# Loading the 64-row remainders of Wq, Wk and Wv over 128 partitions instead of 64

## The chip, the core and the metric

The kernel runs on one core of a Trainium2 chip. The metric is the device time of one execution in microseconds (us). Three executions of the kernel before took 2663.87, 2661.49 and 2657.86 us; the median is 2661.49. A fourth execution was recorded by the hardware profiler; all durations below are from it.

The core has five engines that run their own instruction queues beside each other: TensorE (PE, matrix products; its weight loads are listed as PEld), VectorE (DVE), ScalarE (ACT), GpSimd (POOL) and SyncE (SP). Data come from memory (HBM) through 16 DMA engines, which SP, ACT and POOL feed with transfers. On-chip memory has 128 partitions; a tile's first dimension counts them.

## What is computed

Two pairs of layers over x, which has 2048 rows of 576:

```python
x = x + A(layernorm(x), mem0, Wq, Wk, Wv, Wo)
x = x + B(layernorm(x), w1, w3, w2)
x = x + A(layernorm(x), mem0, Wq, Wk, Wv, Wo)
x = x + B(layernorm(x), w1, w3, w2)
```

`A` is attention over segments of 32 rows. Each segment is put behind a memory of 8 rows, goes through 32 heads of width 128, and its first 8 output rows are the memory of the next segment:

```python
for s in range(n_seg):
    h = concatenate([mem, xs])                # 8 + 32 rows of 576
    q, k, v = h @ Wq, h @ Wk, h @ Wv          # 32 heads of 128 each
    p = softmax(masked(q @ k.T * scale))
    o = (p @ v) @ Wo
    mem = o[:8]; outs.append(o[8:])
```

`B` is a gated feed-forward layer, `(silu(x @ w1) * (x @ w3)) @ w2`, with an inner width of 4608. The weights Wq, Wk and Wv are 576 x 4096 in bfloat16, 4.7 MB each. 576 = 4 x 128 + 64: four chunks of 128 rows and a remainder of 64 rows, 512 KB of each matrix. This remainder is what the change is about.

## The kernel before

The segments are a chain, since each needs the memory of the one before. The kernel walks through 72 steps (64 segments, and the second A layer 8 steps behind the first). In a step, 8 units u of four heads each compute Q and K (QK: the four 128-row chunks; QKt: the 64-row remainder), then scores, softmax, the products with V, and the output product with Wo. FFN work is spread between the steps.

Nothing here is ordered by the hardware alone. `make_nodes` (L232) lists every piece of work with what it depends on; `plan` (L78) puts PE's pieces in the order of a hand-written string of letters (`FIRST`, `FOUR`, `LAST`, L201 to L222: Q is QK, q is QKt) and fits the other engines' work around it. Every instruction of an engine then runs in the order in which the plan emitted it. The lowest-level helpers are `mm` (L632, every matmul), `act` (L635), `v` (L638, every VectorE instruction), `dma` (L641, SP), `adma` (L644, ACT) and `swdma` (L647, POOL), so the profile shows those lines.

The weights are held on chip for the whole run. `T.W` (L1299) has 128 partitions and nine slots of 4096 columns: slots 0 to 3 hold Wq's four chunks, 4 to 7 Wk's, and slot 8 holds both remainders, Wq's 64 rows in partitions 0 to 63 and Wk's 64 rows in partitions 64 to 127. `T.WV` (L1301) holds Wv's chunks and behind them its remainder, which is folded: even blocks of 512 columns in partitions 0 to 63, odd blocks in 64 to 127. The remainder of the activations (`T.HT`, slot 4) is there twice, in both halves of the partitions. So `qk_tail` (L957) can run Q's remainder on the lower and K's on the upper half of PE's rows, as pairs of products of 64 rows each.

Loads at the start, in the order of their queues:

- on ACT: Wk's remainder (64 rows x 8 KB), the first 128 rows of x (XN), mem0 (8 rows), Wv's odd blocks (64 rows x 4 x 1 KB)
- on SP: Wq's remainder (64 rows x 8 KB), Wv's even blocks, then `load_qk` (L693) with the four chunks of the left half of Wq (512 KB each), of Wk's left half, the same of both right halves, `load_v` (L717) with four chunks of 1 MB, `load_o` (L723) with four of 1.15 MB, and the first FFN weights

Each of these transfers signals one of eight semaphores, taken in turn, and a transfer isn't issued before the one eight places earlier has landed. The first step's QK waits for the chunks of Wq and Wk (`ld_h`, L262), its V products for Wv, its output products for Wo.

At the end, the last FFN's weights w1 and w3 are loaded over `T.W` (`tail_load`, L746), 512 columns at a time, after the products of the last step that read those columns (L548); the second and later ones are also held back until named output products.

Of the kernel before, what the change touches and what calls it, by code (L numbers as in the profile page):

```python
# [13 lines left out]
P = 128  # L14
R64 = 64
D = 576
NCH = D // R64
H = 32
E = 128
# [7 lines left out]
NG = 4  # L27
# [204 lines left out]
def make_nodes(em, nseg, pools, o=Opt, dma_bw=230e3, load_bw=345e3):  # L232
# [9 lines left out]
    def banks(n=2):  # L242
        return [Slot("bank") for _ in range(n)]
# [12 lines left out]
    def load(name, nbytes, prio, fn, deps=()):  # L256
        return node("DMA", nbytes / load_bw, fn, deps=deps, prio=prio, name=name, lat=2.0)
# [8 lines left out]
    b = banks(1)  # L266
# [193 lines left out]
    def job(j):  # L460
# [81 lines left out]
        if last:  # L542
            v_done, qk_done = last_reads
            me = steps[nst - 1]
            gates = {1: me["WO1"], **{i: me["WO3"] for i in range(2, 8)}}
            for i in range(8):
                g = gates.get(i)
                tail.append([load("tail", kb(128, c), s0 + o.tail_at + 0.01 * i, em.tail_load(i, what, g), deps=dep + [g])  # L548
                             for what, c, dep in ((0, 9 * 512, qk_done[2 * i:2 * i + 2]), (1, 4 * 576, v_done))])
            shared.pop()()  # L550
        norm()
        if last:
# [29 lines left out]
    for t in range(nst):  # L582
        if t % 4 == 2 and (t + 2) // 4 < ngrp:
            x_in((t + 2) // 4)
        if t == LAG:
            ht_mem[t].append(node("DVE", 0.1, em.init_mem(1, LAG), deps=[m0e] + reads_ht.get(LAG - R_HT, []), prio=LAG - 2, name="m0"))
        if role(t) == 0 or t == 0:
            vx_pair(t - role(t), t - 1 + o.vx)
        step(t)
        if t % 4 == 1 and t // 4 < ngrp:  # L590
            x_res(t // 4)
        if t % 4 == 3:
            job((t + 1) // 4 - 1)
        elif t == nst - 1:
            job(nst // 4)
# [6 lines left out]
SW = 2 * QW  # L602
# [5 lines left out]
class Emitter:  # L608
# [91 lines left out]

    def load_tails(self, what):
        def f(n):
            if what < 2:
                d, wd = (self.dma, self.a.wq) if what == 0 else (self.adma, self.a.wk)
                d(self.T.W[what * R64:(what + 1) * R64, 8, :], wd[4 * P:D, :])
            if what != 1:
                r = what // 2
                (self.adma if r else self.dma)(self.wv(True)[r * R64:(r + 1) * R64, :].rearrange("p (q n) -> p q n", q=NG),
                                               self.a.wv[4 * P:D, :].rearrange("p (q r n) -> r p q n", q=NG, r=2)[r])
        return f  # L710

    def wv(self, tail):
# [227 lines left out]
    def qk(self, t, u, b):  # L940
# [13 lines left out]
                                first and j == 0 and c == 0, c == 3)  # L954
        return f

    def qk_tail(self, t, u, b):  # L957
        def f(n):
            q0, q1 = self.qcols(t)
            HTt = self.ht(t)  # L960
            first = self.begin(b)
            for j in range(4):
                h0 = self.head(u // 2, 4 * (u % 2) + j) * E
                for kind in (0, 1):
                    rr = slice(kind * R64, (kind + 1) * R64)
                    self.mm(self.bk(b[kind])[:, j * SW:j * SW + q1 - q0], self.T.W[rr, 8, h0:h0 + E], HTt[rr, 4, q0:q1],
                            first and j == 0, True, tile_position=(kind * R64, 0))
        return f

    def qk_ev(self, t, u, r, q, b):  # L970
# [420 lines left out]
```

## Time and profile before

| | before |
|---|---|
| median of three executions | 2661.49 us |
| the profiled execution | 2662.86 us |
| its span, from first to last instruction | 2661.1 us |
| PE busy | 2585.4 us (97%) |
| PEld busy | 2228.9 us (84%) |
| DVE busy | 2025.0 us (76%) |
| ACT busy | 1252.0 us (47%) |
| DMA, mean over the span | 140 GB/s |
| DMA in the first of 40 slices (66.5 us) | 321 GB/s |

The page gives the busy time of each engine, then the span in 40 slices, the DMA queues, the chain of work that ended last, and groups of equal instructions. A trace behind it can be asked for a stretch of time: who waited for whom (total, times, longest), the instructions in order of time, the share of the 16 DMA engines that was busy and the rate in GB/s, and how many packets each queue moved. Queue q1 is SP's, q10 is ACT's; a packet is one contiguous piece of a row, and a transfer also ends with small packets, which are counted under 512 B. A share of the DMA engines a little over 100% means that packets overlap on an engine.

### The profile page before, as it was taken

How to read it: one execution, taken by the hardware profiler on the slowest of the kernel's cores; microseconds unless marked ns; L12 is line 12 of the kernel's file. 1: busy time of each engine (PE TensorE's matmuls, PEld its weight loads, DVE VectorE, ACT ScalarE, POOL GpSimd, SP SyncE). 2: the span in 40 equal slices, each digit the busy share in tenths (PEclk: the TensorE clock that was granted, in tenths of full speed). 3: DMA queues.
4: the chain of work that ended last, by engine and by line, in shares of the span. 5: the costliest groups of instructions: out<-in, count | busy, mean ns of one | idle time of the engine just before them, and what ended most of it. 6: DMA issues, size and time to landing. Idle time of an engine off the chain costs nothing.

```text
span 2661.1 us, 134392 instructions
## 1 busy us (share of the span) xinstructions
PE 2585.4 (97%) x59795; PEld 2228.9 (84%) x59795; DVE 2025.0 (76%) x5276; ACT 1252.0 (47%) x3612; POOL 337.1 (13%) x399
## 2 busy tenths in 40 slices
PE   5999999999999999999999999999999999999998
PEld 4788888888888888888888888888888888888887
DVE  4787777787787778777777777777778777777876
ACT  2555453454445444444544444454544445454453
POOL 1111110110111011011101101110111111011110
PEclk8999999999999999999999999999999999999999
DMA  9064845556565556555554655645465564544457
GB/s 321 4 179 123 189 105 149 127 136 148 128 144 105 147 125 145 142 131 147 113 139 116 162 128 141 154 110 136 113 155 125 143 157 101 129 119 128 128 158 236
DMA packets 688135, 371.55 MB, mean 140 GB/s; under 512 B 234072, under 2 KB 682336, under 8 KB 686912
## 3 DMA queue, kind: packets, MB, share of 16 engines
q1 hardware_dynamic: 684016, 355.07, 53.2%
q8 instruction: 467, 7.65, 1.2%
q0 software_dynamic: 3024, 6.93, 0.9%
q10 hardware_dynamic: 512, 0.94, 0.1%
q14 instruction: 116, 0.95, 0.1%
HBM read 306.72 MB, written 2.36 MB: 116 GB/s over the span
## 4 chain that ended last, share of the span: by engine, by line
PE 67%; DMA 7%; DVE 4%; ACT 1%; SPq 1%; issue 1%; POOL 0%; DVEq 0%; POOLq 0%; ACTq 0%
PE bank L632 67%; DMA PTS<-PB 4%; DMA W<-in_B_w_dram 2%; DVE STAT L638 1%; DMA W2C<-in_B_w_dram 1%; DVE SME L638 1%; SPq L641 1%; DVE PB L638 1%; DVE V L638 1%; ACT V L635 0%; DVE XR L638 0%; DVE HTT L638 0%; DVE QKT L638 0%; POOL PB L1052 0%; ACT QKT L635 0%
## 5 line engine op out<-in xcount | busy, mean ns | idle before, releaser
L632 PEld LDWEIGHTS <-W 128*128 128x128 bf16 (+2 forms) x32576 | 1270.4, 101 | 137.4 <-issue 58.6
L632 PE MATMUL bank<-HT,W 128*128 128x80 bf16 (+3 forms) x23040 | 800.0, 197 | 25.9 <-DMA W<-in_A_Wk_dram 8.5
L632 PE MATMUL bank<-XTB,W 128*64 128x256 bf16 (+5 forms) x9536 | 663.2, 263 | 6.3 <-DMA W<-in_B_w_dram 5.9
L1052 POOL MEMSET PB<- 128x1024 bf16 x288 | 273.9, 951 | 1958.6 <-DMA PTS<-PB 1292.0
L635 ACT ACTIVATE QKT<-bank 128x256 bf16<-128x256 f32 (+4 forms) x1456 | 338.9, 310 | 284.6 <-PE bank L632 272.1
L632 PE MATMUL bank<-OT,WO 128*128 128x80 bf16 (+3 forms) x11520 | 417.3, 198 | 1.5 <-issue 0.8
L632 PEld LDWEIGHTS <-WO 128*128 128x128 bf16 (+1 forms) x11520 | 386.2, 102 | 36.8 <-issue 20.9
L635 ACT ACTIVATE V<-bank 64x512 bf16<-64x512 f32 (+1 forms) x625 | 351.7, 585 | 120.2 <-PE bank L632 112.3
L632 PE MATMUL bank<-WV,HT 128*32 128x512 bf16 (+4 forms) x3688 | 370.2, 384 | 1.3 <-DVE HT L638 0.7
L632 PE MATMUL bank<-W2C,HTT 128*64 128x288 bf16 (+1 forms) x3296 | 321.5, 287 | 4.7 <-DMA W2C<-in_B_w_dram 4.7
L635 ACT ACTIVATE OT<-bank 128x320 bf16<-128x320 f32 (+1 forms) x384 | 144.3, 403 | 335.6 <-PE bank L632 332.1
L638 DVE TENSOR_REDUCE STAT<-SME 104x8 f32<-104x320 f32 (+1 forms) x576 | 274.6, 477 | 32.4 <-ACT SME L635 27.0
L638 DVE TENSOR_TENSOR PB<-SME,STAT 40x128 bf16<-40x128 f32 (+4 forms) x912 | 275.5, 336 | 12.2 <-POOL PB L1052 0.4
L638 DVE SCALAR_TENSOR_TENSOR HTT<-HTT,bank 128x512 bf16<-128x512 bf16 (+1 forms) x324 | 201.2, 621 | 105.0 <-ACT HTT L635 101.9
L632 PEld LDWEIGHTS <-HT 128*32 128x32 bf16 (+4 forms) x3688 | 159.0, 100 | 133.3 <-issue 29.7
L632 PEld LDWEIGHTS <-HTT 128*64 128x64 bf16 (+1 forms) x3376 | 230.2, 106 | 42.0 <-issue 8.4
L635 ACT ACTIVATE HTT<-bank 128x512 bf16<-128x512 f32 (+1 forms) x324 | 174.2, 550 | 189.2 <-PE bank L632 187.7
L638 DVE SCALAR_TENSOR_TENSOR XR<-bank,XR 128x288 f32<-128x288 f32 x574 | 242.4, 446 | 18.0 <-PE bank L632 14.9
L635 ACT ACTIVATE SME<-SME 104x320 f32<-104x320 f32 (+1 forms) x288 | 135.2, 469 | 208.1 <-DVE SME L638 205.6
L638 DVE CAST QKT<-bank 128x128 bf16<-128x128 f32 (+2 forms) x592 | 158.2, 315 | 94.5 <-PE bank L632 92.6
L638 DVE TENSOR_TENSOR HTT<-HTT,bank 128x512 bf16<-128x512 bf16 (+1 forms) x324 | 203.5, 628 | 32.5 <-DVE HTT L638 1.4
L638 DVE CAST V<-bank 32x512 bf16<-32x512 f32 (+1 forms) x239 | 163.4, 684 | 33.6 <-PE bank L632 29.4
(59 smaller groups left out, 1414.6 us busy)
## 6 DMA issues: line engine op xcount, KB each, us to landing
W<-in_B_w_dram SPq DMA_DIRECT2D x608, 256.0 KB, 3.9
W2C<-in_B_w_dram SPq DMA_DIRECT2D x304, 288.0 KB, 3.7
W<-in_B_w_dram SPq DMA_DIRECT2D x608, 32.0 KB, 3.8
W<-in_B_w_dram SPq DMA_DIRECT2D x16, 512.0 KB, 8.6
W<-in_A_Wq_dram SPq DMA_DIRECT2D x9, 512.0 KB, 10.2
WO<-in_A_Wo_dram SPq DMA_DIRECT2D x4, 1152.0 KB, 16.7
XR<-in_A_x_dram POOLq DMA_DIRECT2D x16, 288.0 KB, 4.0
WV<-in_B_w_dram SPq DMA_DIRECT2D x8, 576.0 KB, 7.1
```

What stands on the lines that cost most here:

```text
L632: self.ch("PE", self.nc.tensor.matmul(out, lhsT=lhsT, rhs=rhs, start=start, stop=stop, skip_group_check=True, **k))
L635: self.ch("ACT", self.nc.scalar.activation(*a, **k))
L638: self.ch("DVE", getattr(self.nc.vector, fn_)(*a, **k))
L641: self.ch("SP", self.nc.sync.dma_start(out=out, in_=in_))
L1052: return lambda n: self.ch("POOL", self.nc.gpsimd.memset(self.T.PB[:, pb.i], 0.0))
```

## The change

The remainders are loaded in pieces of 128 partitions: one transfer takes two neighbouring blocks of columns of the 64 rows and puts the first into partitions 0 to 63 and the second into 64 to 127. For this the source is read as "h p n": two blocks h, 64 rows p, n columns. The layout of slot 8 changes with it: Wq's remainder takes columns 0 to 2047 in both halves, Wk's columns 2048 to 4095, so that for each unit Q's and K's parts still lie in opposite halves (`qk_tail_at`). Wk's blocks 0 and 3 are still loaded over 64 partitions. Wv's remainder keeps its layout and comes in four transfers. In place of two transfers on SP and two on ACT for the remainders there are four on SP and five on ACT. The loads that overwrite `T.W` at the end depend on the QKt pieces that read the new places.

```diff
@@ make_nodes, the last FFN's loads
-                             for what, c, dep in ((0, 9 * 512, qk_done[2 * i:2 * i + 2]), (1, 4 * 576, v_done))])
+                             for what, c, dep in ((0, 9 * 512, qk_done[2 * i:2 * i + 1] + [me[f"QKt{u}"] for u in range(8) if any(em.qk_tail_at(k, u)[1] == 512 * i for k in (0, 1))]), (1, 4 * 576, v_done))])
@@ load_tails
-            if what < 2:
-                d, wd = (self.dma, self.a.wq) if what == 0 else (self.adma, self.a.wk)
-                d(self.T.W[what * R64:(what + 1) * R64, 8, :], wd[4 * P:D, :])
+            def pair(d, out, wd, at, n):
+                d(out, wd[4 * P:D, at:at + 2 * n].rearrange("p (h n) -> h p n", h=2))
+
+            if what == 0:
+                for i in (0, 1):
+                    pair(self.dma, self.T.W[:, 8, i * 1024:(i + 1) * 1024], self.a.wq, i * 2048, 1024)
+            elif what == 1:
+                self.adma(self.T.W[R64:P, 8, 3072:4096], self.a.wk[4 * P:D, 0:1024])
+                pair(self.adma, self.T.W[:, 8, 2048:3072], self.a.wk, 1024, 1024)
+                self.adma(self.T.W[0:R64, 8, 3072:4096], self.a.wk[4 * P:D, 3072:4096])
             if what != 1:
-                r = what // 2
-                (self.adma if r else self.dma)(self.wv(True)[r * R64:(r + 1) * R64, :].rearrange("p (q n) -> p q n", q=NG),
-                                               self.a.wv[4 * P:D, :].rearrange("p (q r n) -> r p q n", q=NG, r=2)[r])
+                for q in range(what, what + 2):
+                    pair(self.adma if what else self.dma, self.wv(True)[:, q * 512:(q + 1) * 512], self.a.wv, q * 1024, 512)
@@ new function, and qk_tail
+    def qk_tail_at(self, kind, u):
+        i = u // 2
+        block = (3 if i in (0, 3) else 2) if kind else i // 2
+        return R64 * (i % 2 ^ kind), block * 1024 + u % 2 * 512
...
             for j in range(4):
-                h0 = self.head(u // 2, 4 * (u % 2) + j) * E
                 for kind in (0, 1):
-                    rr = slice(kind * R64, (kind + 1) * R64)
-                    self.mm(self.bk(b[kind])[:, j * SW:j * SW + q1 - q0], self.T.W[rr, 8, h0:h0 + E], HTt[rr, 4, q0:q1],
-                            first and j == 0, True, tile_position=(kind * R64, 0))
+                    r0, w0 = self.qk_tail_at(kind, u)
+                    rr = slice(r0, r0 + R64)
+                    self.mm(self.bk(b[kind])[:, j * SW:j * SW + q1 - q0], self.T.W[rr, 8, w0 + j * E:w0 + (j + 1) * E], HTt[rr, 4, q0:q1],
+                            first and j == 0, True, tile_position=(r0, 0))
```

The order of instructions on every engine stays as it was, apart from the loads at the head of SP's and ACT's queues.

## The prediction

> **What bounds the kernel now.** I read the page's busy shares first, then PE's waits by stretch, then the DMA stretches and packet counts of the first 60 us, the only time in which the moved loads run. TensorE (PE) is busy 97% of the span. After 60 us its listed waits add up to some 39 us in 2.6 ms, none of them on Wq, Wk or Wv; before that it waits for these. PE's waits from 13.5 to 58 us:
>
> ```profile
> PE bank L632 <- DMA W<-in_A_Wk_dram: 8.5, 8, 1.1
> PE bank L632 <- DMA W<-in_A_Wq_dram: 4.1, 3, 2.2
> ```
>
> (total us, times, longest.) In time order on PE (start, length, what, idle before it):
>
> ```profile
> 14.85 0.22 PE L632 MATMUL bank<-HT,W 128*128 128x40 bf16 x1 [0.82 <-DMA W<-in_A_Wq_dram]
> 16.13 0.22 PE L632 MATMUL bank<-HT,W 128*128 128x40 bf16 x1 [1.06 <-DMA W<-in_A_Wq_dram]
> 17.41 0.22 PE L632 MATMUL bank<-HT,W 128*128 128x40 bf16 x1 [1.06 <-DMA W<-in_A_Wk_dram]
> 18.70 0.22 PE L632 MATMUL bank<-HT,W 128*128 128x40 bf16 x1 [1.08 <-DMA W<-in_A_Wk_dram]
> ```
>
> One matmul runs each time a 512 KB chunk lands, every 1.28 us: 524,288 B / 1.28 us = 410 GB/s. The DMA stretches (last columns: share of the 16 DMA engines, GB/s) show the same rate, and a slower head:
>
> ```profile
> 2.00:7.00 5.00, 0.00 (x0) 0.00 (x0) 4.30 (x7) 0.00 (x0) 3.67 (x9) 1.00 0.98 225
> 7.00:9.00 2.00, 0.00 (x0) 0.00 (x0) 1.89 (x5) 0.00 (x0) 0.00 (x0) 1.00 1.15 224
> 9.00:13.00 4.00, 0.96 (x15) 0.81 (x16) 1.72 (x8) 1.25 (x1) 0.56 (x1) 1.00 1.04 328
> 14.00:20.00 6.00, 0.92 (x6) 0.45 (x5) 0.00 (x0) 0.00 (x0) 0.00 (x0) 1.00 1.02 407
> ```
>
> The engines are full from 2 us on. The last weight chunk of this queue, WO's fourth, is issued at 44.85 and lands 11.9 us later, at 56.7; PE's WO products run from 51.7 to 57.9 and close the first step. So the stage to 58 us is as long as the load queue: what the queue's head gains or loses reaches step 0's end nearly whole, and as PE's order is written out by hand and it is full from then on, it reaches the end of the kernel.
>
> **What the change does, part by part.** (1) It removes four 64-row transfers (1.573 MB: Wk 512 KB, Wq 512, Wv twice 256). From 2.0 to 13.4 us all queues moved 3.02 MB (the DMA view of that stretch, below); at 407 GB/s that is 7.4 us, so 4.0 us were lost at the head. The four transfers then held the engines 1.573 MB / 407 = 3.9, plus 4.0: **7.9 us**.
>
> (2) It adds seven transfers over 128 partitions (Wq two and Wk one of 256 KB, Wv four of 128 KB: 1,310,720 B) and two of 64 rows (Wk, 128 KB each). What decides is how many DMA engines one of the seven gets. Their source is written "h p n" with h = 2: its outermost step counts two, where every load of before counts 64 or 128 outermost; only the destination counts 128. The trace has one transfer with a small count, mem0's, of 8 rows, on ACT's queue:
>
> ```profile
> DMA packets 1210, 3.02 MB, mean 265 GB/s; under 512 B 120, under 2 KB 768, under 8 KB 1082
> q1 hardware_dynamic: 698, 2.07, 69.6%
> q10 hardware_dynamic: 512, 0.94, 33.6%
> ```
>
> ACT's queue is q10. Its data are Wk's 64 rows of 8 KB, XN's 128 rows, 64 x 4 pieces of 1 KB of Wv and mem0's 8 rows: 456 packets. The other 56 are small closing packets, 56 = 16 + 16 + 16 + 8: each wide transfer was closed by sixteen engines, the 8-row one by eight. So transfers are dealt to engines by their outermost count, and a count under 16 leaves engines out. [...] Each pair is then carried by **two engines**, one half each.
>
> [...]
>
> Price from rows. From 14 to 20 us, 676 packets (80 of them closings) took 102.3% of 16 engines x 6 us: 98.2 us / 596 = 165 ns per 4 KB. From 46.5 to 50.5, 1,353 packets of 1,152 B took 108.6% of 64 us: 51 ns. On the line through both, 2 KB is 86 ns and 1 KB 46 ns. Each of the two engines carries 64 packets per pair: 3 x 64 x 86 = 16.5 us, 4 x 64 x 46 = 11.8 us. The two 64-row transfers give each engine 8 packets of 2 KB; at the head's pace (8 KB in some 560 ns from 2 to 6.9 us, a quarter of it 0.14 us) 1.2 us. New: **29.5 us** on two engines against 7.9 on all: **+21.6 us**. All later chunks need all 16 engines, so they land at the pace of these two.
>
> Bounds: at the pace of 8 KB packets alone on the engines (from 32 to 38 us 301 of them, beside 18 of 4 KB, took 101.8% of 96 us: 315 ns, 26.0 GB/s an engine) 25.2 + 0.65 - 7.9 = +18. At ACT's 1 KB packets from 10 to 12.8 us (202 in 24.9% of 44.8 us: 55 ns, and twice that for 2 KB) 21.1 + 14.1 + 1.2 - 7.9 = +28.5. [...]
>
> (3) New waits. The loads take eight semaphores in turn; mem0 and the two Wv pairs of ACT are now ninth to twelfth and wait, in ACT's queue, for the first Wq pair, the Wk pair and the second Wq pair. Behind them on ACT stand the table load and the copies into HT (11.74 to 14.0 us now). On two engines the second Wq pair is done around 20 to 24 us; HT would follow some 3 us later, XN's own load by 25 at the latest. PE's first full product would start with Wq's first chunk at 29 to 36 us and its first unit end with Wk's fourth chunk, at 21.2 + 21.6 = 43. So these waits lie under the loads: nothing. Without that cover (sixteen engines) the second Wq pair ends by 6 to 7 us, before XN's landing at 8.4: nothing again. Five more issues at 0.35 to 0.6 us lie under the transfers.
>
> (4) QKt (L957) reads the other half for u = 2, 3, 6 and 7, K opposite. The trace's pairs start 3 ns apart and 32 ns after the pair before, in both halves at once; that stays. Where a unit with the other order follows directly, one matmul could wait for its half: written order has 84 such places, so at most 84 x 32 ns = 2.7 us; I take nothing, the nearest row being a pair that already waits 32.
>
> (5) The last FFN's loads over W wait for other QKt. SP's order is unchanged. The first such load is issued at 2594.9 to 2597.4, when six units' QKt of the last step run (2594.98, 48 matmuls); the next at 2609.9, after all of them. Nothing; at worst the first loads slip 1 us, with SP idle till 2599.3 behind.
>
> Sum: the profiled execution took 2662.86 us (span 2661.1 and 1.8 around it), 1.4 above the median 2661.49. 2662.86 + 21.6 = 2684.5, on the median's level 2683.1; I forecast **2684**.
>
> **Rivals.** *Sixteen engines after all (faster, within measurement).* If the destination's 128 rows deal the transfer, the head runs at full width: of the 4.0 us lost, 0.55 stays with the two 64-row Wk transfers (0.26 MB at 225 instead of 407 GB/s) and 0.3 with smaller packets: -3.1 us, 2659.8, on the median's level 2658. For it: 225 GB/s with the engines 98% busy, next to 407. It decides at the outermost count: if the source's 2 doesn't limit. Against: mem0's eight closings. [...]
>
> *Two engines, but another two for each transfer.* Then the busiest engine has one pair, 64 x 86 = 5.5 us, and 1.2: 6.7 instead of 7.9, about -1 us: 2661 to 2662. The packet counts can't show which engines are used.
>
> *Two engines, and part of the delay lost.* PE's granted clock is 0.61 from 32 to 40 us; another start could run at another clock, 2 us either way. It lies inside the range.
>
> **Chances.** Two engines, always the same: 0.80. Sixteen: 0.12. Changing couples: 0.05. Anything else slower: 0.03. The range holds the first: +18 and +28.5 on 2661.5, with 3 us for the spread of the runs (2657.86 to 2663.87): 2676 to 2693. A measurement of this kernel tells 0.2%, 5.3 us, from no change; sixteen engines give -3.1, mostly within it: faster 0.02, same 0.15, slower 0.83.
>
> **What would show it.** Right: from 2 to 30 us a DMA share near 2/16 in long stretches and a mean under 120 GB/s; two closing packets per pair; Wk's fourth chunk used near 43 us, WO's last product near 79; all later rows as before, 22 us later. Wrong: 400 GB/s from the start, with the first full product before 13 us (sixteen engines), or Wk's fourth chunk at 20 to 22 (changing couples). An end that moves without the 58 us mark moving would refute parts 4 and 5.

## The result, and the profile after

The changed kernel took 2682.18 us (median of four executions, 2680.11 to 2683.95); the kernel before took 2660.84 (four, 2657.86 to 2663.87). The ratio is 1.0082, 95% interval 1.0070 to 1.0095: slower by 21.3 us on the medians. The profiled execution took 2683.95 us (span 2682.2), 21.1 more than that of before. The forecast was 2684, in a range of 2676 to 2693.

The stretches of the changed kernel (last three columns: PE's granted clock, share of the 16 DMA engines, GB/s):

```profile
2.00:7.00 5.00, 0.00 (x0) 0.00 (x0) 4.30 (x7) 0.00 (x0) 3.67 (x9) 1.00 0.51 108
7.00:9.00 2.00, 0.00 (x0) 0.00 (x0) 1.34 (x3) 0.00 (x0) 0.00 (x0) 1.00 0.13 51
14.00:20.00 6.00, 0.00 (x0) 0.00 (x0) 0.94 (x3) 0.00 (x0) 0.00 (x0) 1.00 0.13 50
36.00:42.00 6.00, 0.86 (x4) 0.42 (x4) 0.00 (x0) 0.00 (x0) 0.00 (x0) 1.00 0.98 356
```

A share of 0.13 is 2.1 of 16 engines, and they move 50 GB/s where before moved 407 in the same stretch. The DMA view of 14 to 20 us tells more:

```profile
DMA packets 169, 0.30 MB, mean 50 GB/s; under 512 B 9, under 2 KB 37, under 8 KB 169
q1 hardware_dynamic: 108, 0.21, 9.1%
q10 hardware_dynamic: 61, 0.09, 4.1%
```

Both queues, SP's q1 and ACT's q10, have a pair in flight here, and together they fill 13.2% of the engines. With another couple for each transfer it would be four engines, 25%. So it is the same two. The page's row of ACT's queue counts the closing packets:

```profile
q10 hardware_dynamic: 710, 0.94, 0.1%
```

Its data are 64 + 128 + 64 rows of Wk, 128 of XN, 8 of mem0 and 2 x 128 of Wv: 648. The other 62 are 16 each for the three wide transfers, 8 for mem0 and 2 for each of the three pairs. PE in time order (start, length, what, idle before):

```profile
24.13 0.32 PE L632 MATMUL bank<-HT,W 64*128 64x40 bf16 x8 [1.64 <-ACT HT L635]
33.47 0.22 PE L632 MATMUL bank<-HT,W 128*128 128x40 bf16 x1 [9.02 <-DMA W<-in_A_Wq_dram]
35.15 0.22 PE L632 MATMUL bank<-HT,W 128*128 128x40 bf16 x1 [1.47 <-DMA W<-in_A_Wq_dram]
...
43.32 3.51 PE L632 MATMUL bank<-HT,W 128*128 128x40 bf16 x97 [1.08 <-DMA W<-in_A_Wk_dram]
```

Before, the last of these rows was:

```profile
21.24 3.51 PE L632 MATMUL bank<-HT,W 128*128 128x40 bf16 x97 [1.05 <-DMA W<-in_A_Wk_dram]
```

The activations are ready at 24, but Wq's first chunk is used at 33.47 and Wk's fourth at 43.32; before used the latter at 21.24, so the step is 22.1 us late. PE's waits from 13.5 to 80 us put 12.5 us on Wq where before had 4.1:

```profile
PE bank L632 <- DVE XN L638: 21.5, 1, 21.5
PE bank L632 <- DMA W<-in_A_Wq_dram: 12.5, 4, 9.0
PE bank L632 <- DMA W<-in_A_Wk_dram: 8.0, 7, 1.5
```

The 21.5 (counted from the span's start) are the wait for XN, the first rows of x. That load has 128 rows and so sixteen shares, two of which stand behind the pairs (fourteen of its closings come by 6.84 us, the last two at 18.13 and 19.01; 16 of its rows' packets still run after 14 us): issued at 3.03, it lands at 19.01, where before had it at 8.4. This costs nothing of its own, since Wq comes later still. The step ends with WO's products, last start at 79.1 (57.9 before). The changed kernel's row, then before's:

```profile
L632 PE MATMUL bank<-OT,WO x160: 179/202/243, 70.8 to 79.1; 128*128 128x40 bf16 x128, 128*64 128x40 bf16 x32
L632 PE MATMUL bank<-OT,WO x160: 179/186/243, 51.7 to 57.9; 128*128 128x40 bf16 x128, 128*64 128x40 bf16 x32
```

From there the same instructions of the two traces lie 21 to 25 us apart to the end.

### The profile page after: what moved, and what is told of

Read it like the earlier page. It is cut to its first block, busy times and chain, and to the rows that moved or that the text cites. A ratio compares the mean times of both kernels' runs of the same rounds, so it can differ in the third digit from the quotient of the medians.

```text
span 2682.2 us, 134396 instructions
## 1 busy us (share of the span) xinstructions
PE 2584.9 (96%) x59795; PEld 2230.1 (83%) x59795; DVE 2024.8 (75%) x5276; ACT 1253.4 (47%) x3612; POOL 337.4 (13%) x399
## 4 chain that ended last, share of the span: by engine, by line
PE 81%; DMA 9%; DVE 5%; ACT 2%; SPq 1%; issue 1%; POOL 0%; DVEq 0%; POOLq 0%; ACTq 0%
PE bank L632 81%; DMA PTS<-PB 5%; DMA W<-in_B_w_dram 2%; SPq L641 1%; DVE V L638 1%; DVE SME L638 1%; DVE STAT L638 1%; ACT V L635 1%; DMA W<-in_A_Wk_dram 1%; DVE HTT L638 1%; DMA W<-in_A_Wq_dram 1%; DVE PB L638 1%; DMA W2C<-in_B_w_dram 1%; ACT QKT L635 0%; DVE XR L638 0%
## 5 line engine op out<-in xcount | busy, mean ns | idle before, releaser
L632 PE MATMUL bank<-HT,W 128*128 128x80 bf16 (+3 forms) x23040 | 801.3, 197 | 34.2 <-DMA W<-in_A_Wq_dram 12.5
L632 PEld LDWEIGHTS <-WO 128*128 128x128 bf16 (+1 forms) x11520 | 386.8, 102 | 38.5 <-issue 22.5
```

Of the source, the lines that this page charges most:

```text
L632: self.ch("PE", self.nc.tensor.matmul(out, lhsT=lhsT, rhs=rhs, start=start, stop=stop, skip_group_check=True, **k))
```

## The experiments

**Theory:** the transfers' outermost count of two leaves each pair to the same two engines, and the 21 us are the time of their packets. **Rivals:** the new places of the remainders (QKt, the late loads), the number of transfers, or the new waits on ACT hold up the start. Each set has its own runs of the kernel before: their medians are 2660.12 us (25 runs) for the first four kernels, 2657.59 (29) for the next three and 2657.54 (7) for the last.

**1. Each pair cut into two transfers of 64 partitions.** Places, order and bytes stay; the outermost count becomes 64.

```diff
-                d(out, wd[4 * P:D, at:at + 2 * n].rearrange("p (h n) -> h p n", h=2))
+                for h in (0, 1):
+                    d(out[h * R64:(h + 1) * R64], wd[4 * P:D, at + h * n:at + (h + 1) * n])
```

> Each paired transfer of the changed kernel is cut in two transfers of 64 partitions, lower then upper; places, QKt, the later dependencies and the wait rules stay as changed. Theory (each pair is carried by two DMA engines because the source's outermost step counts two): all 16 engines work again, the remainders take 6 to 9 us instead of 29.5, Wk's fourth chunk is used at 19 to 22 us (43.3 in the changed kernel), time within 3 us of the kernel before (2658 to 2664), about 20 us under the changed one. Rival (the loss comes from the new places in W, from QKt's halves or from the new waits on ACT, not from how a transfer is dealt out): still 2676 to 2684, and Wk's fourth chunk after 35 us.

Measured: 2664.92 us (11 runs), ratio 1.0013, interval 1.0003 to 1.0023. The stretches:

```profile
2.00:7.00 5.00, 0.00 (x0) 0.00 (x0) 4.30 (x7) 0.00 (x0) 3.67 (x9) 1.00 0.92 236
7.00:9.00 2.00, 0.00 (x0) 0.00 (x0) 1.89 (x5) 0.00 (x0) 0.00 (x0) 1.00 0.62 138
14.00:20.00 6.00, 0.86 (x4) 0.41 (x4) 0.00 (x0) 0.00 (x0) 0.00 (x0) 1.00 1.01 395
```

With the same places, nearly all of the 0.82% is gone: the delay comes neither from the places nor from the late loads, but from the paired form of the transfers. (Cutting a pair changes its partitions and the number of transfers as well as the outermost count; experiment 2 changes the count alone.) Wk's fourth chunk is used at 23.48, later than expected. The engines have a hole at 7 to 9 us (share 0.62): eight short transfers, where before had two, now stand ahead of Wq's first chunk on SP, which is issued at 8.53 (2.27 in before). A remainder of 0.13% is left; experiments 5 and 6 look for it.

**2. The same pairs with the rows outermost.** The source count becomes 64. The data of a row then land in two neighbouring partitions, so the remainders are not where the products look for them; that other values cost no time is assumed, here and in experiments 3 and 7.

```diff
-                d(out, wd[4 * P:D, at:at + 2 * n].rearrange("p (h n) -> h p n", h=2))
+                d(out, wd[4 * P:D, at:at + 2 * n].rearrange("p (h n) -> p h n", h=2))
```

> The paired transfers read their source as p h n instead of h p n: the same bytes, rows, packets, partitions and issues, only the source's outermost step counts 64 instead of 2. [...] Theory (outermost count): 16 engines, full rate from the start (near 400 GB/s from 3 us on), the head's loss of 4 us mostly gone: Wk's fourth chunk used near 18.2 us, time 1 to 4 us under the kernel before, 2657 to 2660 where it runs at 2661. Rival (the pattern with a third dimension is slow to issue, whatever its order): as the changed kernel, 2680 to 2684. Second rival (128 partitions win nothing over 64): as before within 1 us, Wk's fourth chunk at 21 us.

Measured: 2665.82 us (11 runs), ratio 1.0018, interval 1.0008 to 1.0029. Neither the delay nor the gain that I expected is there. Its stretches:

```profile
2.00:7.00 5.00, 0.00 (x0) 0.00 (x0) 4.30 (x7) 0.00 (x0) 3.67 (x9) 1.00 0.93 254
7.00:9.00 2.00, 0.00 (x0) 0.00 (x0) 1.85 (x5) 0.00 (x0) 0.00 (x0) 1.00 1.05 337
30.00:36.00 6.00, 4.38 (x115) 3.96 (x115) 1.53 (x6) 0.79 (x3) 0.96 (x1) 0.50 1.02 425
52.00:60.00 8.00, 6.11 (x170) 5.78 (x169) 1.15 (x5) 1.28 (x5) 1.62 (x2) 0.50 1.04 281
```

The head is better than before's: 254 and 337 GB/s where before had 225 and 224. Wk's fourth chunk is used 1.0 us earlier (20.20), and from 32 to 56 us the kernel is 2.4 to 3.0 us ahead of before. At 59 us no more than 0.3 us of it is left, and from 64 to 200 us mostly 0.6 to 0.7. From 52 to 60 us PE stands once before WO, and its clock is 0.50 throughout, against 0.79 in before's same stretch. PE's row, then before's stretch and row:

```profile
54.90 2.86 PE L632 MATMUL bank<-OT,WO 128*128 128x40 bf16 x80 [1.41 <-issue]
52.00:60.00 8.00, 7.41 (x243) 7.04 (x240) 2.10 (x9) 1.81 (x8) 2.48 (x3) 0.79 0.92 270
55.85 2.23 PE L632 MATMUL bank<-OT,WO 128*128 128x40 bf16 x80
```

Before ran this block of 80 in 2.23 us, 0.6 less, and did not stand before it. So the width of the transfer alone is not what costs: 128 partitions with 64 rows outermost give back all but 0.18% of 0.82%. How most of the lead of 2.5 us is lost is seen in one profile, as a stop of 1.41 us and a lower clock; that the earlier start brings these about was not tried. It is not the whole of the 0.18%: from 500 us on this trace lies 1.0 to 5.5 us behind before, for which I have no cause, and experiment 1's trace, too, wanders after 60 us, between 2.5 us ahead of before and 2.2 behind.

**3. Four engines.** Count four: 32 rows by four column blocks. The upper 32 rows of the remainders are not loaded and other columns stand in their places, so a part of Q, K and V is computed from wrong weights.

```diff
-                d(out, wd[4 * P:D, at:at + 2 * n].rearrange("p (h n) -> h p n", h=2))
+                at = 0 if n == 1024 else at % 2048
+                d(out, wd[4 * P:4 * P + 32, at:at + 4 * n].rearrange("p (h n) -> h p n", h=4))
```

> The paired transfers take four blocks of 32 rows instead of two of 64: the same bytes, packets and partitions, source's outermost count 4 (the upper 32 rows are left out and other columns stand in their place, so the products of the remainders differ). Theory: four engines, each with 32 packets per transfer: 3 x 32 x 86 ns + 4 x 32 x 46 ns = 14.1 us, with the 1.2 us of the two 64-row ones 15.3 instead of 7.9: 6 to 9 us over the kernel before, 2667 to 2670; DMA share near 4/16 in the head; Wk's fourth chunk near 28.6 us. Rival (engines change from transfer to transfer, or the cost is per transfer and not per engine): over 2677 or under 2664.

Measured: 2673.52 us (4 runs), ratio 1.0049, interval 1.0035 to 1.0063: 13 us over before, more than expected; Wk's fourth chunk is used at 31.31, not near 28.6. The share of engines while only such transfers run is the one expected of four engines, 4/16; the excess lies elsewhere. From 30 to 36 us the engines are not full:

```profile
7.00:9.00 2.00, 0.00 (x0) 0.00 (x0) 1.34 (x3) 0.00 (x0) 0.00 (x0) 1.00 0.27 102
30.00:36.00 6.00, 4.69 (x143) 4.47 (x144) 1.33 (x5) 0.91 (x3) 0.00 (x0) 1.00 0.60 186
```

and SP's waits to 45 us say for what:

```profile
SPq L641 <- DMA WV<-in_A_Wv_dram: 13.9, 4, 6.2
```

SP waits for pairs of Wv whose semaphores it takes again for later chunks, ACT's two among them, which ACT issued late, behind its own wait. Experiment 7 takes this away.

**4. Before, with Wv alone in pairs.** Wq and Wk stay as they were.

```diff
...
+                for q in range(what, what + 2):
+                    (self.adma if what else self.dma)(self.wv(True)[:, q * 512:(q + 1) * 512],
+                                                      self.a.wv[4 * P:D, q * 1024:(q + 1) * 1024].rearrange("p (h n) -> h p n", h=2))
```

> The kernel before with one part of the change alone: Wv's remainder in four paired transfers; Wq, Wk, W's places and QKt as before. Theory: 4 x 64 x 46 ns = 11.8 us on the same two engines in place of some 3 us on all: 7 to 11 us over the kernel before, 2668 to 2672. Rival (each transfer gets another couple of engines): 2.9 us on each couple, within 1 us of before. Rival (places and QKt cost the time): within 1 us of before.

Measured: 2669.52 us (8 runs), ratio 1.0033, interval 1.0018 to 1.0047: some 9 us, as expected. Four of the seven pairs, with 40% of the paired bytes, make about 40% of the delay (0.33 of 0.82%; by the interval 0.18 to 0.47), without any new place for Wq and Wk.

**5. The new places alone.** Slot 8 has the changed layout, with QKt and the last FFN's dependencies as changed; the loads go over 64 partitions, in few transfers.

```diff
-            def pair(d, out, wd, at, n):
-                d(out, wd[4 * P:D, at:at + 2 * n].rearrange("p (h n) -> h p n", h=2))
+            def half(d, out, wd, r):
+                d(out.rearrange("p (q n) -> p q n", q=2), wd[4 * P:D, :].rearrange("p (q r n) -> r p q n", q=2, r=2)[r])
...
```

> The new places in W, QKt's new halves and the last FFN's new dependencies, with loads like those of before: 64 partitions, rows of 2 KB, two transfers for Wq, three for Wk, two for Wv. It asks for the price of the places alone, which the cut-up pairs left at 0.13% together with their 16 transfers. Theory (places and QKt's halves cost nothing, part 4 of the prediction): within 2 us of before. Rival (QKt's unlike neighbours and the later dependencies cost): 3 to 5 us over before, spread over the steps.

Measured: 2657.62 us (12 runs), ratio 0.9998, interval 0.9989 to 1.0008. The places cost nothing, to within some 3 us either way.

**6. The pieces alone.** Before's places, the remainders in 16 transfers of 64 partitions.

```diff
-                d(self.T.W[what * R64:(what + 1) * R64, 8, :], wd[4 * P:D, :])
+                for c in range(0, 4096, 1024):
+                    d(self.T.W[what * R64:(what + 1) * R64, 8, c:c + 1024], wd[4 * P:D, c:c + 1024])
...
```

> The kernel before with its places, and the remainders in the same 16 transfers of 64 partitions as the cut-up pairs (four each for Wk and Wq, eight for Wv). Theory (the 0.13% of the cut-up pairs come from the number of transfers at the head, which moves Wk's fourth chunk from 21.2 to 23.5 us): 2 to 4 us over before, Wk's fourth chunk near 23.5. Rival (the places cost it): within 1 us of before.

Measured: 2658.71 us (12 runs), ratio 1.0006, interval 0.9993 to 1.0018. Wk's fourth chunk is used at 22.15, 0.9 us after before's and not at the 23.5 expected of the theory. From 2 to 7 us these transfers of 64 partitions, with XN's beside them as in experiment 2, move as much as experiment 2's of 128:

```profile
2.00:7.00 5.00, 0.00 (x0) 0.00 (x0) 4.30 (x7) 0.00 (x0) 3.68 (x9) 1.00 0.92 256
```

Neither places nor pieces by themselves can be told from no change, so where the 0.13% of experiment 1 comes from stays open.

**7. Four engines, all pairs of Wv on SP.** Experiment 3, with Wv's four transfers ahead of Wq's first chunk on SP and none on ACT.

```diff
-            if what != 1:
-                for q in range(what, what + 2):
-                    pair(self.adma if what else self.dma, self.wv(True)[:, q * 512:(q + 1) * 512], self.a.wv, q * 1024, 512)
+            if what == 0:
+                for q in range(NG):
+                    pair(self.dma, self.wv(True)[:, q * 512:(q + 1) * 512], self.a.wv, q * 1024, 512)
```

> The kernel with four blocks of 32 rows (products of the remainders differ as there), but all four Wv transfers on SP ahead of Wq's first chunk, none on ACT. With four engines it took 13.4 us over before where 7.4 were worked out, and SP's issue of Wk's fourth chunk (24.67) and Wq's next (31.18) stood behind the landing of ACT's two Wv transfers, whose semaphores they take. Theory (that wait is the difference): the loads no longer stall, Wk's fourth chunk near 29 us, time 6 to 9 us over before. Rival (four engines cost 13 us by themselves): as with the two on ACT, 12 to 14 us over before, and Wk's fourth chunk at 31 us.

Measured: 2663.21 us (10 runs), ratio 1.0021, interval 1.0009 to 1.0034: 5.6 us, where experiment 3 had 13, and a little under the 6 to 9 expected. Wk's fourth chunk is used at 30.30, only 1.0 us before experiment 3's and not near 29; the gain comes behind it. The stretch in which experiment 3 had a share of 0.60 is full, and SP's waits for Wv are short:

```profile
30.00:36.00 6.00, 5.34 (x156) 5.06 (x157) 2.23 (x6) 1.44 (x6) 0.00 (x0) 1.00 1.03 411
```
```profile
SPq L641 <- DMA WV<-in_A_Wv_dram: 5.1, 4, 1.5
```

So with four engines the waits through ACT cost some 7 us (13.4 less 5.6, each known to within 4). The prediction held such waits to be free in the changed kernel; the last experiment asks that.

**8. The changed kernel, all pairs of Wv on SP.** The edit of experiment 7 on the changed kernel, two engines.

> The changed kernel with one difference: all four pairs of Wv are issued by SP ahead of Wq's first chunk, and none by ACT behind mem0, so that nothing on ACT waits for a semaphore of SP's pairs. The seven pairs are the same and still go out on two engines each. Theory A (the new waits of part 3 lie under the loads and cost nothing; the delay is the two engines' own 29.5 us): the median stays 19 to 22 us over before, Wk's fourth chunk is used at 42 to 44 us. Theory B (as with four engines, where the waits on ACT's late pairs took some 7 us of the 13, in the changed kernel too the stall through ACT is a part of the delay): 13 to 17 us over before, Wk's fourth chunk at 36 to 39 us. Between them, 17 to 19 us, a part of it.

Measured: 2675.61 us (4 runs), ratio 1.0071, interval 1.0044 to 1.0098, 18.1 us over before. That lies between the ranges of the two theories, and the interval, 12 to 26 us, doesn't tell them apart. The trace says more. Its stretch and PE's line for Wk's fourth chunk:

```profile
14.00:20.00 6.00, 0.00 (x0) 0.00 (x0) 1.18 (x4) 0.00 (x0) 0.40 (x1) 1.00 0.13 50
```
```profile
41.92 3.51 PE L632 MATMUL bank<-HT,W 128*128 128x40 bf16 x97 [1.07 <-DMA W<-in_A_Wk_dram]
```

41.92 is 1.4 us before the changed kernel's 43.32, just under theory A's 42 to 44 and far from the 36 to 39 of a stall. 0.5 us of it is there at Wq's first chunk (32.97 instead of 33.47), the rest comes from chunks that now land every 1.28 us where the changed kernel has gaps up to 1.7. At two engines the waits lie under the pairs but for some 1.4 us at the first unit, in one profile of each. At the step's end it is 2.6 us (WO's last product starts at 76.5 instead of 79.1); how much of that is the clock's stays open.

## Why the prediction was right

**Parts 1 and 2, the sum.** Right in kind and size. The price per packet fits: from 14 to 20 us the trace has 132 packets of 2 KB, 18 of 1,152 B and 10 of 1 KB, which took 84.8, 52 and 46 ns in the mean; the prediction's line has 86, 51 and 46. By these, 132 x 86 + 18 x 51 + 10 x 46 ns = 12.73 us, and 13.2% of 96 us are 12.67. The pairs' last packet, on ACT's queue, ends at 34.99, 33.0 after the head's start at 2.0. Among the pairs' packets the two engines also carried their shares of XN (8 x 52 ns) and of Wq's first two chunks (16 x 165 ns; landed at 33.42 and 35.11), together 3.1 us. That leaves 29.9; forecast 29.5. From 22.5 to 30 us (share 0.67) the other fourteen engines do their shares of Wq's first chunks, but each chunk lands only when the two get to it: of the first, fourteen closings come from 24.49 to 25.16 and the last two at 31.49 and 33.42; it is used at 33.47, the seven others 1.2 to 1.7 us apart, "at the pace of these two", as forecast. Wk's fourth chunk at 43.32 (forecast near 43) and WO's last product at 79.1 (near 79) follow; the mean from 2 to 30 us is 108 GB/s, under the 120 named.

That the source's count of two alone limits the transfer, which the forecast takes and no row of before showed, is now shown: two closings per pair; a share of 0.27 (four of 16 are 0.25) at count four, in experiment 3 from 7 to 9 us; 0.93 and 1.05 in experiment 2, with the same 128 partitions. Nor did a row of before show that all seven pairs go to the same two engines, on which the 29.5 us rest; the share of 0.13 shows it for the pairs in flight together, and the 29.9 us left above fit it for all seven. Which two of the sixteen they are is not shown.

**Part 3, the waits.** "Nothing" was nearly right for the changed kernel: by experiment 8's profile 1.4 us at the first unit and 2.6 at the step's end. The cover named for it was the right one, the two engines themselves. The prediction named only the waits in ACT's queue. SP's own chunks waited as well, 9.7 us in three waits for pairs of Wv, under the same cover; and an issue, priced at 0.35 to 0.6 us, lasted up to 8 (last section). Nor did it see what the waits do when the cover gets thinner: at four engines they cost 7 us.

**Parts 4 and 5, places and last loads.** Right, to within some 3 us: experiment 5, 0.9998.

**The rivals.** Changing couples are refuted by the share of 0.13. "Sixteen engines after all" did not happen, and experiment 2 shows what it would have given: a head of 254 and 337 GB/s, and 0.18% more time, not the 3.1 us less of the forecast for it. That what the head gains or loses "reaches step 0's end nearly whole" held for the loss of 22 us and not for this gain: of 2.4 to 3.0 us no more than 0.3 are left at 59 us. The forecast for it has the head's 225 GB/s rise to 407 with 128 partitions; no run shows that the number of partitions sets that rate. Before's head already wrote both halves, Wq's remainder on SP's queue into the lower and Wk's on ACT's into the upper, and experiment 6 moves 256 GB/s there in transfers of 64 partitions. From 7 to 9 us experiment 2 moves 337 GB/s and before 224, but other loads run in both stretches, and no run here takes the width by itself.

**The clock.** The 22.1 us at the first unit fall to 19 between 36 and 56 us of before's time, where before itself waited 2.23 us for a late Wq chunk and the changed kernel doesn't, and come back to 22 by 64 us, where the changed kernel's PE runs at 0.57 from 70 to 90 us and before's at 1.00 from 60 to 90. The prediction's "2 us either way" for the clock was about that size; that the two nearly cancel was luck, not working.

## What to carry to other kernels

Before widening a load, look at the outermost count of both sides, not at the partitions: a rearranged source that counts two outermost left 128 partitions to two engines, and the closing packets of each queue (total minus data rows; on ACT's queue here 710 less 648, with two for each pair) tell the number from a profile. Each pair as two transfers of 64 partitions (ratio 1.0013) cost nearly nothing here, as one paired transfer (1.0082) 21 us for the seven. A fuller head of the load queue is worth only what the step's end keeps of it: 254 and 337 GB/s in place of 225 and 224 did not make this kernel faster.

## What had not been expected of the hardware

**The issue of one transfer lasted 8.03 us and held back those behind it.** SP's issues in the changed kernel, in time order (start, length, transfers):

```profile
2.20 15.29 SPq L641 DMA_DIRECT2D WV<-in_A_Wv_dram  x2
17.53 14.60 SPq L641 DMA_DIRECT2D W<-in_A_Wq_dram  x4
```

The second of the two Wv issues starts at 9.46 and Wq's first chunk's only at 17.53, though the semaphore that it takes was free at 3.57. In experiment 8, SP spends 20.57 us on four such issues, and none of its waits for a semaphore in its first 60 us is longer than 1.8. So in the changed kernel fourteen idle engines could not begin on Wq's chunks until 22.5 us (share 0.13 from 7 us until then). It isn't few engines as such. Before has it with WO's four transfers, on sixteen engines:

```profile
30.93 16.79 SPq L641 DMA_DIRECT2D WO<-in_A_Wo_dram  x4
```

The second of these issues lasts from 32.20 to 40.94. What the two have in common is 64 packets an engine: 128 pieces of a pair on two, 1,024 rows of 1,152 B of WO on sixteen. What holds the issue was not measured by itself.

**PE's half clock came in pieces of 3.41 us.** In before's trace the granted clock falls to 0.50 six times for 3.41 us and once for 10.24, three times as long; in the changed kernel's four times for 3.41, once each for 6.83 and 17.07, two and five times as long, and for 1.81 at the trace's end. Counted as time lost (half of the time at 0.50), the first 90 us hold 8.5 us of it before, 13.7 in the changed kernel, 13.7 in experiment 2, 8.5 in experiments 1 and 5; the ten traces range from 6.8 to 13.7. That spread of 6.9 us is more than the 2.4 to 3.0 us by which experiment 2's earlier loads led; whether an earlier start brings more of it was not tried.
